# Pooled attention into a gated feed-forward layer: scores and main value products as single float32 matmuls, two product chains for the first tiles, a third weight buffer

## The chip, the core and the metric

The kernel runs on one core of a Trainium2 chip. TensorE (PE in the profile) multiplies: it holds a stationary operand of up to 128x128 and streams the columns of a moving operand past it, into PSUM. VectorE (DVE), ScalarE (ACT) and GpSimd (POOL) do the elementwise work; the SP queue issues all transfers between memory and SBUF. The metric is the device time of one execution in microseconds (us), as the median of the runs; it is compared with runs of the kernel before on the same chip.

## The reference

```python
def _attn_ref(q, k, v):                      # B, H, S, D = 8, 8, 576, 64
    k_p = k.reshape(B, H, 72, 8, D).mean(axis=3)
    v_p = v.reshape(B, H, 72, 8, D).mean(axis=3)
    scores = matmul(q, k_p.transpose(0, 1, 3, 2)) / sqrt(D)
    attn = exp(scores - max(scores))
    attn = attn / (sum(attn) + 1e-09)
    return matmul(attn, v_p)

x = attn_out.transpose(0, 2, 1, 3).reshape(4608, 512)
a, b = x @ w_a, x @ w_b                      # 512 x 1536 each
out = (a * b) @ w_out                        # 1536 x 512
```

All inputs are float32, and the weights arrive as 64-bit words that the kernel turns back into float32.

## The kernel before

**Tiles.** The 4608 rows of x are cut into 36 chunks of 128 rows, 18 blocks of 256 and 9 tiles of 512. A chunk goes through attention: scores (`psc`), softmax on DVE and ACT (`m`, `s`, `z`, `pr`), transposes on TensorE (`ptr`, `ptr_rem`); a block then has its value products (`po`), which are x transposed. The 64 first of the 72 pooled keys go through `vdiag`, the last 8 through `vrem`. A batch has 576 rows, so six of the 18 blocks lie in two batches, and so do chunks such as chunk 4. Keys and values of a batch are pooled by TensorE for batches 0 and 1 (`pkp`, `pvp`, true float32 matmuls with a matrix of eighths), by DVE otherwise.

**Feed-forward.** For each tile t and each of 12 slices f of the 1536 inner columns there is an inner product (`in`: `psa` and `psb`, 24 matmuls of 512 columns) and an outer one (`out`: `acc`, 12 matmuls). Tiles 0, 1 and 2 are done plainly; the pairs (3,4), (5,6), (7,8) with seven products in place of eight (`both`, banks `bank_psa`, `bank_psb`, `bank_att`).

**Split parts.** TensorE's float32r format keeps less of a number than float32. So each operand is split into a high part (a float32r copy, made by ACT) and a low part (the difference, made by DVE or POOL), and each product is three matmuls: high with high, high with low, low with high. This holds for the feed-forward products, and in the kernel before also for the scores (`qh`, `ql` from `qraw`; `kdiag` with two parts) and the main value products (`p0`, `p1`, in the first block `early_p`; `vdiag` with two parts).

**Weights.** For each f the words of w_a, w_b and w_out come in (`words`, 512 KB each), are converted in place on ACT and DVE (L500 to L520), split into `jab` (a and b) and `jo_open` (w_out), and the split parts are stored to memory (`jd`, `od`) for the later tiles. `jab` has two buffers, taken in turn.

**Order.** The order on each engine is made in advance by a list scheduler in the program (`Schedule`, with costs per operation): chains of operations are spawned with a rank, and among the operations that are ready on an engine at about the same planned time the lowest rank goes first. All feed-forward products of all tiles are one chain, `main`, in a fixed list `order`: in(0,f), then out(0,f-1), from f = 5 on with in(1,f) between them. On the chip each engine works strictly through its own list, and TensorE too starts its matmuls in that order. POOL may take a subtraction from DVE only after planned time `ALONE` (150 us), and when DVE's planned backlog exceeds `HELP`.

Of the kernel before, what the change touches and what calls it, by code (L numbers as in the profile page):

```python
# [17 lines left out]
POOL = 8  # L18
SP = S // POOL
P = 128  # L20
# [17 lines left out]
NTMP = 5  # L38
# [6 lines left out]
JOIN, STEP = 40, 8  # L45
# [16 lines left out]
MARGIN, HELP, AHEAD_F = 1.5, 1.5, 2  # L62
ALONE = 150.0
# [134 lines left out]
def attn_moe_kernel(ctx: ExitStack, tc: tile.TileContext, q, k, kn, v, vn, vr, wa, wb, wo, out):  # L198
# [79 lines left out]
    def pe(calls, rank=None, turn=False, passes=1):  # L278
        cost = 0.0
        for n, (to, lhs, rhs, *_) in enumerate(calls):  # L280
            cols = max(size(to), 64 if passes > 1 else 0) * passes
            other = n + 1 == len(calls) or (calls[n + 1][1].name, calls[n + 1][1].offset) != (lhs.name, lhs.offset)
            cost += max(COLUMN * cols, 0.075 if turn else 0.112 if other else 0.064)
# [25 lines left out]
    def xslot(x, name):  # L309
        return place(sb, [P, NK * NT], F32R, f"x{x}", name)  # L310
# [14 lines left out]
    work = place(sb, [P, 3 * 1024], I32, "work", "words")  # L325
    area = {"ab": work[:, :2048], "o": work[:, 2048:]}
# [11 lines left out]
    early_p = {x: xslot(x // 2, f"early_p{x}") for x in (0, 2)}  # L338
# [5 lines left out]
    jab = [jab_at(4 + x, f"jab{x}") for x in range(2)]  # L344
# [11 lines left out]
    def claim(tag):  # L356
        yield lambda: tag in banks
        banks.remove(tag)

# [243 lines left out]
    def sums_of_weights():  # L603
        yield W(*(("weight", name, NF - 1) for name in ("ab", "o")))
        three = place(sb, [P, 3, NK * BLOCK], F32R, "work", "sums")
        for f in range(NF):
            hi, lo = three[:, 2], three[:, f % 2]
# [129 lines left out]
    kv, qs = ["kv0", "kv1"], ["qraw"]  # L737
# [29 lines left out]
    def summed_keys(b):  # L767
        yield W(("keys", b - 1, 2), ("constants",))
        kd, tag = kdiag[b % 2], None
        for j in range(NK + 1):  # L770
            yield lambda: ("k", b, j) in raws
            if not j:
                tag = yield from take(banks)
                pt = bank(tag, f"pkp_{b}")[:, :NK * SP].rearrange("p (g s) -> p g s", g=NK)
# [5 lines left out]
            ], passes=4)  # L780
            kv.append(kv_of["k", b, j])
        for g0 in range(0, NK, 2):
            gs = slice(g0, g0 + 2)
            for e in range(2):
                r = slice(e * D, e * D + D)
                yield act(
                    kd[r, gs, 0, e, :], pt[r, gs], lambda r=r, e=e, gs=gs: nc.scalar.mul(kd[r, gs, 0, e, :], pt[r, gs], SCALE)
                )
            for e in range(2):
                r = slice(e * D, e * D + D)  # L790
                yield stt(kd[r, gs, 1, e, :], pt[r, gs], SCALE, kd[r, gs, 0, e, :].bitcast(F32), ALU.mult, ALU.subtract)
# [3 lines left out]
    def summed_values(b):  # L795
# [3 lines left out]
        for j in range(NK + 1):  # L799
            yield lambda: ("v", b, j) in raws  # L800
            rows, raw = rows_in(j), raws["v", b, j]
            if j in (0, NK):
                tag = yield from take(banks)
                pt = bank(tag, f"pvp_{b}_{j}")
            if j < NK:
                yield pe([(pt, main_of[:, j].rearrange("p e s -> p (e s)"), raw[:, :DM], not j, j == NK - 1)], passes=4)
            else:
# [5 lines left out]
                ], passes=4)  # L813
            if b:
                kv.append(kv_of["v", b, j])
            if j == NK - 1:
                by_pair = pt.rearrange("p (g e d) -> p g e d", g=NK, e=2)
                for e in range(2):
                    r = slice(e * KM, e * KM + KM)
                    yield copy(vd[r, :, 0, r], by_pair[r, :, e])  # L820
                for e in range(2):
                    r = slice(e * KM, e * KM + KM)
                    yield low_part(vd[r, :, 1, r], by_pair[r, :, e], vd[r, :, 0, r])
# [9 lines left out]
    def load_keys(b):  # L833
# [6 lines left out]
        for g0 in range(0, NK, 2):  # L840
# [10 lines left out]
            for e in range(2):  # L851
                r = slice(e * D, e * D + D)
                yield act(
                    kd[r, gs, 0, e, :], kp[r, gs],
                    lambda r=r, e=e: nc.scalar.mul(kd[r, gs, 0, e, :], kp[r, gs], SCALE / POOL),  # L855
                )
            for e in range(2):
                r = slice(e * D, e * D + D)
                yield stt(
                    kd[r, gs, 1, e, :], kp[r, gs], SCALE / POOL, kd[r, gs, 0, e, :].bitcast(F32), ALU.mult, ALU.subtract  # L860
                )
# [3 lines left out]
    def load_values(b):  # L865
# [12 lines left out]
        for e in range(2):  # L878
            r = slice(e * KM, e * KM + KM)
            yield act(  # L880
                vd[r, :, 0, r], vp[r, :NK], lambda r=r: nc.scalar.mul(vd[r, :, 0, r], vp[r, :NK], 1.0 / POOL)
            )
# [14 lines left out]
        for e in range(2):  # L897
            r = slice(e * KM, e * KM + KM)
# [529 lines left out]
```

## Time and profile before

| | before |
|---|---|
| median of 3 runs | 1019.37 us (1017.39 to 1020.46) |
| profiled execution | 1019.52 us |
| its span, first to last instruction | 1017.7 us |
| TensorE busy | 995.0 us (98%) |
| weight loads of TensorE busy | 829.3 us (81%) |
| VectorE busy | 623.9 us (61%) |
| ScalarE busy | 408.9 us (40%) |
| GpSimd busy | 172.0 us (17%) |
| mean granted TensorE clock | 0.983 |

TensorE's row is the one to read closely: a busy share of 98% does not tell at which clock it was busy, nor whether a matmul was bound by its columns or by the load of its stationary operand. Times of the prediction are counted against the profiled execution, which lies 0.15 us above the median.

### The profile page before, as it was taken

Reading aid. Unit: us, or ns where it says so; the run is one execution under the profiler, and the core shown is the slowest. Engines: PE = TensorE matmul, PEld = TensorE weight load, DVE = VectorE, ACT = ScalarE, POOL = GpSimd, SP = SyncE. Lnnn points to the kernel's source line nnn. Section 1 sums busy time; section 2 is a strip of 40 time slices with the busy share of each in tenths; the row PEclk is TensorE's granted clock in tenths of the full one; section 3 lists DMA queues with packets and bytes.
Section 4 is the critical chain, followed back from the end, with each engine's and each line's share of the span. In section 5 each row is a group of like instructions: output and inputs, shape, how many; then the busy total and the mean of one; then the engine's idle time right before and its main releaser. Section 6 shows DMA issues by size and latency. Waiting matters only on the chain.

```text
span 1017.7 us, 13575 instructions
## 1 busy us (share of the span) xinstructions
PE 995.0 (98%) x4824; PEld 829.3 (81%) x4824; DVE 623.9 (61%) x1018; ACT 408.9 (40%) x832; POOL 172.0 (17%) x139
## 2 busy tenths in 40 slices
PE   6889999999999999999999999999999999999998
PEld 5768888888888888888888887888888787888876
DVE  6697898889887885688776428333333733333331
ACT  5577755645465553544434215211111521111131
POOL 2000003201111110022212115022222502222210
PEclk9598999999999999999999999999999999999999
DMA  6396698798989789687775677666667967666792
GB/s 237 125 333 219 239 314 303 259 316 322 308 266 300 247 298 326 224 270 245 245 242 178 212 264 281 226 197 213 222 208 273 343 222 264 210 216 216 237 348 80
DMA packets 120659, 255.70 MB, mean 251 GB/s; under 512 B 10192, under 2 KB 26576, under 8 KB 120592
## 3 DMA queue, kind: packets, MB, share of 16 engines
q1 hardware_dynamic: 120592, 254.84, 74.3%
q8 instruction: 38, 0.62, 0.2%
q14 instruction: 29, 0.24, 0.1%
HBM read 195.30 MB, written 59.51 MB: 250 GB/s over the span
## 4 chain that ended last, share of the span: by engine, by line
PE 91%; DMA 4%; DVE 2%; ACT 1%; issue 0%; SPq 0%; POOL 0%; ACTq 0%
PE acc L291 28%; PE bank_psb L291 14%; PE bank_psa L291 10%; PE bank_att L291 9%; PE psa L291 9%; PE psb L291 9%; PE psc L291 5%; PE po L291 4%; PE ptr L288 1%; DMA words<-in_wb 1%; DMA j<-jd 1%; PE pvp L291 1%; PE pkp L291 1%; DMA kraw<-in_k 1%; DMA wo_first<-in_k 0%
## 5 line engine op out<-in xcount | busy, mean ns | idle before, releaser
L291 PE MATMUL bank_psb<-x,j 128*128 128x512 f32 x648 | 165.8, 391 | 0.8 <-DMA j<-jd 0.8
L291 PEld LDWEIGHTS bank_psb<-x,j 128*128 128x128 f32 x648 | 120.5, 188 | 26.2 <-DVE temp L234 1.2
L291 PE MATMUL acc<-jo_later,hh 128*128 128x512 f32 x384 | 121.3, 397 | 0.3
L291 PE MATMUL bank_psa<-x,j 128*128 128x512 f32 x432 | 110.8, 392 | 0.0
L291 PE MATMUL bank_att<-x,j 128*128 128x512 f32 x432 | 110.7, 391 | 0.0
L234 DVE TENSOR_TENSOR temp<-bank_psb,temp 128x512 f32<-128x512 f32 x72 | 49.8, 692 | 86.3 <-PE bank_psb L291 86.2
L291 PE MATMUL psa<-xh,jab 128*128 128x512 f32 x288 | 100.5, 402 | 0.0
L291 PE MATMUL psb<-xh,jab 128*128 128x512 f32 x288 | 99.3, 397 | 0.0
L291 PEld LDWEIGHTS bank_att<-x,j 128*128 128x128 f32 x432 | 80.3, 188 | 16.9 <-issue 0.4
L291 PEld LDWEIGHTS bank_psa<-x,j 128*128 128x128 f32 x432 | 80.3, 188 | 16.5
L234 DVE TENSOR_TENSOR temp<-bank_att,temp 128x512 f32<-128x512 f32 x54 | 37.3, 692 | 77.3 <-PE bank_att L291 74.9
L234 DVE TENSOR_TENSOR temp<-bank_psa,temp 128x512 f32<-128x512 f32 x54 | 37.3, 691 | 74.8 <-PE bank_psa L291 73.8
L291 PEld LDWEIGHTS acc<-jo_later,hh 128*128 128x128 f32 x384 | 69.5, 188 | 13.8 <-ACT hh L256 1.6
L234 POOL TENSOR_TENSOR temp_p<-temp_p,temp 128x512 f32<-128x512 f32 x36 | 46.9, 1302 | 194.2 <-ACT temp_p L256 189.2
L234 POOL TENSOR_TENSOR temp_h<-temp_h,temp 128x512 f32<-128x512 f32 x36 | 47.8, 1327 | 176.9 <-ACT temp_h L256 166.6
L291 PE MATMUL acc<-jo_later,hl 128*128 128x512 f32 x192 | 75.5, 393 | 0.6 <-DVE hl L234 0.6
L256 ACT CAST hh<-temp 128x512 fp32r<-128x512 f32 x36 | 22.4, 621 | 113.6 <-DVE temp L234 113.6
L291 PE MATMUL psc<-kdiag,qh 128*128 128x144 f32 x320 | 60.0, 283 | 8.2 <-ACT kdiag L855 8.0
L291 PEld LDWEIGHTS psc<-kdiag,qh 128*128 128x128 f32 x320 | 55.4, 200 | 14.8 <-POOL wab L442 8.0
L291 PEld LDWEIGHTS psa<-xh,jab 128*128 128x128 f32 x288 | 55.6, 193 | 11.3
L291 PE MATMUL acc<-jo_open,hh 128*128 128x512 f32 x192 | 61.9, 404 | 1.7 <-DVE wab L241 1.7
L291 PEld LDWEIGHTS psb<-xh,jab 128*128 128x128 f32 x288 | 54.1, 188 | 10.6
(156 smaller groups left out, 1850.1 us busy)
## 6 DMA issues: line engine op xcount, KB each, us to landing
j<-jd SPq DMA_DIRECT2D x108, 512.0 KB, 5.5
jo_later<-od SPq DMA_DIRECT2D x48, 512.0 KB, 3.7
wo<-od SPq DMA_DIRECT2D x36, 512.0 KB, 6.5
jab<-jd SPq DMA_DIRECT2D x34, 512.0 KB, 6.1
jd<-jab SPq DMA_DIRECT2D x24, 512.0 KB, 4.8
jd<-sums SPq DMA_DIRECT2D x24, 512.0 KB, 4.2
back<-later SPq DMA_DIRECT2D x43, 256.0 KB, 5.2
out<-y SPq DMA_DIRECT2D x36, 256.0 KB, 5.8
```

The source lines that it names most:

```text
L234: run = lambda e: vec[e].tensor_tensor(out=out, in0=in0, in1=in1, op=op)
L256: return act(out, in_, lambda: nc.scalar.copy(out, in_), rank)
L288: nc.tensor.transpose(to, lhs, rhs)
L291: nc.tensor.matmul(to, lhs, rhs, start=start, stop=stop, skip_group_check=bool(skip))
```

## The change

Three things are changed, and several numbers of the planner with them.

- Scores and main value products are one float32 matmul each, where three float32r matmuls stood. `qh`, `ql`, the low part of `kdiag`, the low part of `vdiag` and the low part of the transposed probabilities are gone, with the ACT copies of `q` and the DVE and POOL subtractions that made them. The products of the last 8 pooled keys (`vrem`) stay as they are.
- The products of tiles 0 and 1 are taken out of `main` into two chains: `first_ins` (inner products) and `first_outs` (outer products, with the better rank). `main` waits for the first and goes on with tile 2.
- `jab` has a third buffer. The raw q has three buffers in place of one, and there are 7 in place of 5 temporary tiles. The words of a and b and those of w_out get tiles of their own.

```diff
-NTMP = 5
+NTMP = 7
-JOIN, STEP = 40, 8
+JOIN, STEP = 40, 7
-MARGIN, HELP, AHEAD_F = 1.5, 1.5, 2
-ALONE = 150.0
+MARGIN, HELP, AHEAD_F = 1.5, 2.5, 2
+ALONE = 60.0
...
-    kdiag = [const.tile([P, NK, 2, 2, SP], F32R, name=f"kdiag{i}") for i in range(2)]
-    vdiag = [const.tile([P, NK, 2, P], F32R, name=f"vdiag{i}") for i in range(2)]
+    kdiag = [const.tile([P, NK, 2, SP], F32, name=f"kdiag{i}") for i in range(2)]
+    vdiag = [const.tile([P, NK, P], F32, name=f"vdiag{i}") for i in range(2)]
...
-    jab = [jab_at(4 + x, f"jab{x}") for x in range(2)]
+    jab = [jab_at(x, f"jab{n}") for n, x in enumerate((4, 5, 7))]
...
-        yield copy(qh, qraw)
-        yield low_part(ql, qraw, qh, (SG, SV))
...
                 yield pe([
-                    (
-                        pt[:, j * hk:(j + 1) * hk], qq[:, g0 + j], kd[:, g0 + j, w].rearrange("p e s -> p (e s)"),
-                        x == 0, x == 2,
-                    )
-                    for j in range(2) for x, (qq, w) in enumerate(((qh, 0), (qh, 1), (ql, 0)))
+                    (pt[:, j * hk:(j + 1) * hk], turned_q[:, g0 + j], kd[:, g0 + j].rearrange("p e s -> p (e s)"), True, True)
+                    for j in range(2)
                 ])
...
         yield copy(th[:, :, here], pt)
-        yield low_part(tl[:, :, here], pt, th[:, :, here])
...
-                        (vdiag[b % 2][:, g, 0, :], th[:, g, lo:hi], True, False),
-                        (vdiag[b % 2][:, g, 0, :], tl[:, g, lo:hi], False, False),
-                        (vdiag[b % 2][:, g, 1, :], th[:, g, lo:hi], False, False),
+                        (vdiag[b % 2][:, g], th[:, g, lo:hi], True, False),
...
+    def first_ins():
+        yield W(*(("value", block_of[i]) for i in range(NCH) if tile_of[i] == 0))
+        yield from claim("psa", "psb")
+        for kind, t, f in order:
+            if kind != "in" or t > 1:
+                continue
+            if t:
+                yield W(*(("value", block_of[i]) for i in range(NCH) if tile_of[i] == 1))
+            else:
+                mark("begun", f)
+            yield from ffn_in(t, f)
+            mark("issued", "in", t, f)
+        mark("first_ins")
+
+    def first_outs():
+        for kind, t, f in order:
+            if kind == "out" and t < 2:
+                yield from ffn_out(t, f)
+        ...
...
-        sch.spawn(main(), 1e9)
+        sch.spawn(first_outs(), 1e9)
+        sch.spawn(first_ins(), 2e9)
+        sch.spawn(main(), 2e9)
```

**Where the order changes.** Three places are shown, before and after. A name carries the chunk, block or batch and then a piece number, so `psc_4_2` is the second half of the scores of chunk 4, and `pvp_1_0` sums the values of batch 1 out of `vraw_1_0` to `vraw_1_3`; the last number of a name only keeps buffers apart.

On TensorE, before, the last value products of tile 0 are followed at once by the first inner product:

```order
L291 MATMUL po_1_2_488<-p0_1_427,vdiag0_79 128x256
L291 MATMUL po_1_2_488<-p2_1_429,vrem_0_214 128x256
L291 MATMUL psa_0_0_506<-xh_0_85,jab0_87 128x512
L291 MATMUL psa_0_0_506<-xl_0_86,jab0_87 128x512
L291 MATMUL psa_0_0_506<-xh_0_85,jab0_87 128x512 x2
```

The value sums of batch 1 and the scores of chunk 4 stand behind the inner product psa_0_1 there. On TensorE after, at the same place:

```order
L292 MATMUL po_1_2_423<-p2_1_369,vrem_0_193 128x256
L292 MATMUL pvp_1_0_432<-vraw_1_0_358,wab2_75 128x512
L292 MATMUL psc_4_0_428<-kdiag1_78,q_4_182 128x144 x2
L292 MATMUL pvp_1_0_432<-vraw_1_1_389,wab2_75 128x512
L292 MATMUL psc_5_0_429<-kdiag1_78,q_5_226 128x144 x2
L292 MATMUL psc_5_2_455<-kdiag1_78,q_5_226 128x144 x2
L292 MATMUL psc_4_2_465<-kdiag0_77,q_4_182 128x144 x2
L292 MATMUL psc_4_2_471<-kdiag1_78,q_4_182 128x144 x2
L292 MATMUL psc_6_0_478<-kdiag1_78,q_6_265 128x144 x2
L292 MATMUL psc_6_2_482<-kdiag1_78,q_6_265 128x144 x2
L292 MATMUL pvp_1_0_432<-vraw_1_2_440,wab2_75 128x512
L292 MATMUL pvp_1_0_432<-vraw_1_3_452,wab2_75 128x512
```

The main value sums of batch 1 and the scores of chunks 4, 5 and 6 moved ahead of the first inner product, which is the next row (psa_0_0).

On DVE, before, around the second half of tile 0 (`p1` is a low part that is gone after; `wab0` is the weight slice f = 0 until `jab0` is written, then f = 1; `xl` is the low part of x):

```order
L234 ISA wab0_73<-wab0_73,wlow_b0_283 128x1024
L245 TENSOR_SCALAR wo_first_72<-wo_first_72 128x512
L241 SCALAR_TENSOR_TENSOR wo_first_72<-words_82,wo_first_72 128x512
L234 TENSOR_TENSOR p1_1_428<-ptr_3_451,p0_1_427 128x4x128
L234 ISA wo_first_72<-wo_first_72,wlow_o0_322 128x1024
L234 TENSOR_TENSOR jab0_87<-wab0_73,jab0_87 128x2x512
L245 TENSOR_SCALAR wab0_73<-wab0_73 128x1024
L234 TENSOR_TENSOR xl_0_86<-po_1_0_472,xh_0_85 128x2x256
```

and after:

```order
L234 ISA wab0_73<-wab0_73,wlow_b0_336 128x1024
L245 TENSOR_SCALAR wo_first_72<-wo_first_72 128x512
L241 SCALAR_TENSOR_TENSOR wo_first_72<-words_o_83,wo_first_72 128x512
L234 ISA wo_first_72<-wo_first_72,wlow_o0_366 128x1024
L234 TENSOR_TENSOR jab0_88<-wab0_73,jab0_88 128x2x512
L234 TENSOR_TENSOR xl_0_87<-po_1_0_411,xh_0_86 128x2x256
```

The low part of the probabilities is gone between the weight steps, and the conversion of f = 1 moved behind the x of tile 0.

On the SP queue, before, the transfers around the first stores of split weights:

```order
L271 DMA jd0_90<-jab0_87 256x1x512
L271 DMA od0_102<-jo_open_89 128x1024
L271 DMA jd1_91<-jab1_88 256x1x512
L271 DMA words_82<-in_wo 128x1024
L271 DMA qraw_5_555<-in_q 128x512
L271 DMA vraw_1_2_591<-in_vn 128x512
L271 DMA jd1_91<-jab1_88 256x1x512
L271 DMA vraw_1_3_603<-in_vn 128x512
```

and after:

```order
L271 DMA vraw_1_1_389<-in_vn 128x512
L271 DMA words_o_83<-in_wo 128x1024
L271 DMA jd0_92<-jab0_88 256x1x512
L271 DMA od0_104<-jo_open_91 128x1024
L271 DMA vraw_1_2_440<-in_vn 128x512
L271 DMA vraw_1_3_452<-in_vn 128x512
```

The third and fourth value transfers of batch 1 moved ahead of the stores of f = 1, and stand right behind the first store of w_out's split parts (od0).

## Rows read from the trace of the kernel before

**Rows 1.** The page: TensorE's granted clock in 40 slices of the span, tenths.

```profile
PEclk9598999999999999999999999999999999999999
```

**Rows 2.** Busy time by stretch: PE, PEld, DVE, ACT, POOL, PEclk, DMA share, GB/s.

```profile
0.00:25.00 25.00, 16.14 (x74) 12.77 (x75) 17.27 (x37) 14.61 (x41) 6.47 (x19) 0.97 0.69 241
25.00:50.00 25.00, 21.33 (x93) 19.41 (x92) 16.83 (x34) 14.61 (x41) 0.00 (x0) 0.50 0.35 122
50.00:75.00 25.00, 22.21 (x110) 16.89 (x108) 22.48 (x40) 17.29 (x38) 0.00 (x0) 0.98 0.99 334
75.00:100.00 25.00, 23.31 (x123) 19.71 (x123) 19.84 (x37) 18.97 (x53) 0.00 (x0) 0.87 0.63 204
100.00:1000.00 900.00, 898.05 (x4372) 749.34 (x4371) 546.08 (x871) 339.83 (x655) 165.57 (x120) 1.00 0.77 258
```

**Rows 3.** The same view, of the two stretches at half clock.

```profile
23.60:50.90 27.30, 23.63 (x102) 21.52 (x102) 19.07 (x38) 15.96 (x44) 0.00 (x0) 0.50 0.34 116
74.80:81.60 6.80, 5.11 (x15) 3.75 (x14) 5.98 (x14) 4.98 (x17) 0.00 (x0) 0.50 0.57 203
```

**Rows 4.** The chain that ended last: start us, us, what, matmul records.

```profile
48.41 3.96 PE psa L291 x12
52.37 2.72 PE psb L291 x12
...
63.62 0.63 PE psc L291 x6
...
65.68 0.86 PE pvp L291 x2
...
90.38 1.76 PE po L291 x16
...
98.11 0.44 PE ptr L288 x4
...
114.32 0.12 PE ptr_rem L288 x2
...
117.25 0.95 PE po L291 x8
```

**Rows 5.** TensorE's groups by shape: count, busy us, mean ns, idle before and releaser.

```profile
L291 PE MATMUL psc<-kdiag,qh 128*128 128x144 f32 x320 | 60.0, 283 | 8.2 <-ACT kdiag L855 8.0 <-ACT xo L256 0.2
L291 PE MATMUL psc<-kdiag,ql 128*128 128x144 f32 x160 | 46.0, 287 | 0.9 <-DVE ql L234 0.9
L291 PE MATMUL po<-p,vdiag 128*128 128x256 f32 x132 | 23.9, 296 | 1.2 <-ACT p L256 0.8 <-DVE p L234 0.4
```

**Rows 6.** Timeline of TensorE in the opening: start us, us, what, records.

```profile
10.59 0.63 PE L291 MATMUL psc<-kdiag,qh 128*128 128x144 f32 x2
11.01 0.41 PE L291 MATMUL psc<-kdiag,ql 128*128 128x144 f32 x1
11.23 0.63 PE L291 MATMUL psc<-kdiag,qh 128*128 128x144 f32 x2
...
20.45 1.06 PE L291 MATMUL pkp<-eighth,kraw 128*128 128x16 f32 x8
21.37 0.42 PE L291 MATMUL psc<-kdiag,qh 128*128 128x144 f32 x2
```

**Rows 7.** Timeline of DVE in the opening, idle time and releaser in brackets.

```profile
33.06 0.69 DVE L234 TENSOR_TENSOR xl<-po,xh 128x512 fp32r<-128x512 f32 x1 [3.32 <-ACT xh L256]
38.39 0.69 DVE L234 TENSOR_TENSOR xl<-po,xh 128x512 fp32r<-128x512 f32 x1 [2.97 <-ACT xh L256]
```

**Rows 8.** Timeline of TensorE from 72 to 77 us.

```profile
74.38 0.69 PE L288 MATMUL ptr<-ident,pr 128*128 128x128 f32 x4 [2.54 <-DVE s L234]
76.75 0.79 PE L291 MATMUL acc<-jo_open,hh 128*128 128x512 f32 x1 [1.69 <-DVE wab L241]
```

**Rows 9.** Groups of DVE, ACT and POOL that the change removes: count, busy us, mean ns.

```profile
L234 DVE TENSOR_TENSOR p<-ptr,p 128x512 fp32r<-128x512 f32 x34 | 23.4, 689 | 17.4 <-ACT p L256 17.3
L256 ACT CAST qh<-qraw 128x512 fp32r<-128x512 f32 x32 | 19.9, 622 | 6.4 <-PE psc L291 3.6 <-DMA qraw<-in_q 2.5
L234 POOL TENSOR_TENSOR ql<-qraw,qh 128x512 fp32r<-128x512 f32 x19 | 26.0, 1369 | 114.4 <-ACT qh L256 88.5 <-PE po L291 16.6 <-DVE vdiag L241 5.6
```

**Rows 10.** Transfers issued from 25 to 100 us: count, KB each, median us to landing.

```profile
words<-in_wb SPq DMA_DIRECT2D x5, 512.0 KB, 5.2
vraw<-in_vn SPq DMA_DIRECT2D x4, 256.0 KB, 4.2
```

More of the change, by code (lines that the diff above doesn't have):

```diff
@@ L276, in until_ready, with pe @@
         return op
-    def pe(calls, rank=None, turn=False, passes=1):
+    def pe(calls, rank=None, turn=False):
         cost = 0.0
         for n, (to, lhs, rhs, *_) in enumerate(calls):
-            cols = max(size(to), 64 if passes > 1 else 0) * passes
+            exact = lhs.dtype == F32 and not turn
             other = n + 1 == len(calls) or (calls[n + 1][1].name, calls[n + 1][1].offset) != (lhs.name, lhs.offset)
-            cost += max(COLUMN * cols, 0.075 if turn else 0.112 if other else 0.064)
+            floor = 0.225 if exact else (0.109 if lhs.dtype == F32 else 0.061) if turn else 0.111 if other else 0.068
+            cost += max(COLUMN * size(to) * (4 if exact else 1), floor)
         def run(e):
@@ L819, in summed_values @@
                     r = slice(e * KM, e * KM + KM)
[L820 to L823, printed above, removed]
+                    yield copy(vd[r, :, r], by_pair[r, :, e])
                 banks.append(tag)
@@ L853, in load_keys @@
                 yield act(
[L854 to L860, printed above, removed]
+                    kd[r, gs, e], kp[r, gs], lambda r=r, e=e: nc.scalar.mul(kd[r, gs, e], kp[r, gs], SCALE / POOL)
                 )
@@ L896, in load_values @@
         yield copy(vrf[:NR], wide[:NR])
-        for e in range(2):
-            r = slice(e * KM, e * KM + KM)
-            yield stt(vd[r, :, 1, r], vp[r, :NK], 1.0 / POOL, vd[r, :, 0, r].bitcast(F32), ALU.mult, ALU.subtract)
         r = slice(2 * 4 * KR, NR)
@@ L957, in chunk @@
                     banks.append(tag)
+        if not first:
+            qs.append(tag_q)
         for n, (tag, four) in enumerate(held_banks):
@@ L1308, in both @@
         waiting.extend(ffn_out(t0, f, (c,)) for c in range(NT // P))
+    def first_ins():
[15 more added lines that the diff above has]
+                yield from ffn_out(t, f)
+        jo.append(place(sb, [P, 4 * 512], F32R, "jo", "jo_later").rearrange("p (k h c) -> p k h c", k=2, h=2))
+        mark("first_outs")
     def main():
+        yield W(("first_ins",))
         for kind, t, f in order:
[L1312 to L1321 removed]
+            if kind == "in" and t > 1:
+                yield W(("whole", t))
                 yield from ffn_in(t, f)
                 mark("issued", "in", t, f)
[L1324 removed]
+            elif kind == "out" and t > 1:
+                yield W(("first_outs",))
                 yield from ffn_out(t, f)
[L1326 to L1327 removed]
             elif kind == "both":
                 yield from both(t, f)
[L1330 removed]
+            elif kind == "rest":
                 while waiting:
```

105 lines of the change are left out of this document (42 added, 63 removed).

## The prediction

> **What bounds the kernel now.** I read the busy time by stretch first, because a share of 98% over the whole span says nothing about single stages. From 100 to 1000 us TensorE is busy 898.05 of 900 us at a granted clock of 1.00 [rows 2]: there only the price of its own matmuls counts, and what the other engines are spared costs or gains nothing as long as they stay ahead (DVE 546 of the 900 us, ACT 340). The first 100 us are another matter: TensorE is busy 16.1, 21.3, 22.2 and 23.3 of 25 us each, and in two stretches, 23.6 to 50.9 and 74.8 to 81.6 us, at half clock [rows 1 to 3]. I then read the chain that ended last for the price of a matmul, as start to start in a row of its kind: 12 feed-forward matmuls take 2.72 us, so 0.227 each; six score matmuls 0.63, so 0.105; a float32 value sum (pvp, two records of 512 columns) 0.86; eight value matmuls of 256 columns 0.95; sixteen of a block in two batches 1.76; four transposes 0.44, two small ones 0.12 [rows 4]. The mean durations of single matmuls (283 ns for a score) are no price, since matmuls overlap [rows 5]. Three terms follow: TensorE's own work, the opening up to the first inner product, and the stretch after it.
>
> **Term 1, TensorE's own work.** Scores: 480 matmuls now, in 80 groups of six [rows 5], at 0.63: 50.4 us. After, 160 float32 matmuls of 144 columns. The trace has float32 matmuls at two sizes. At 512 columns one takes 0.86, that is 1.68 ns a column, which gives 0.242 for 144. At 16 columns eight records (four matmuls) take 0.92 us from 20.45 to 21.37, so 0.23 a matmul [rows 6]; this is the floor, and 0.242 lies just above it. 160 x 0.242 = 38.7: a gain of 11.7 us. Bounds: the score stays at 0.242 if load and stream overlap as in these rows; some 0.01 for changing between kinds would leave 10.
>
> Here a rule of the Trainium skill speaks against the change. By the row, three float32r matmuls of 144 columns take 0.315, and the width sets little of it, as 256 columns take hardly more (0.95/8 = 0.119) [rows 4]. The Trainium skill's page FP8 and Floating Point Precision, section TensorE Precision Notes, says that true float32 takes four passes through the array, so by columns alone four passes replace three. By that count three matmuls would cost 3 x 144 x 0.227/512 = 0.19, and the change would lose about 8 us on the scores in place of gaining 11.7. The trace agrees on the four passes (0.86 against 0.227 for 512 columns) but not on the count by columns, and the Trainium skill's page TensorE: Matmul & The Clock Gate, section LDWEIGHTS (loading the stationary operand), has the reason: a load of the stationary operand takes time by its own 128 columns, an estimate of 107 ns by its formula, whatever streams past it. Since the rows price the three matmuls directly, the count by columns gets no chance of its own below.
>
> Value products: 12 blocks lie in one batch. There a group of two head pairs has eight matmuls at 0.95; after it has two float32 ones at 256 x 1.68 ns = 0.43 and two for the rest at 0.119, 1.10 in all: +0.15 x 24 = +3.6 us. In the six blocks with two batches sixteen matmuls take 1.76; after, pieces of 64 and 128 columns cost the floor of 0.23 and 192 columns 0.32, and the rest 0.11 each: 1.54 (64 with 192, four blocks) or 1.36 (128 with 128, two). That is -0.22 x 8 - 0.40 x 4 = -3.4. Together nothing. Term 1 is -11.7, say -12, between -9 and -13.
>
> **Term 2, the opening.** The first inner product (psa) starts at about 48.2 us [rows 4]. TensorE began at 8.0, when the first kdiag was there [rows 5], and waits and half clock filled the rest. After, TensorE's list ahead of psa is at full clock: 32 score matmuls 7.7, eight value sums of 512 columns 6.9 and four small ones 0.9, 20 key sums 4.6, four chunks of transposes 2.2, eight head pairs of value products at 0.55 4.4; 26.7 us. Of this, 7.3 us (four value sums, 16 score matmuls) stood behind the first psa before. So the term is the shift of psa plus 7.3.
>
> When does psa start? With TensorE never waiting: 8.0 + 26.7, and 4.4 more since it ran at half rate up to some 17 us (three scores in 0.64 at 10.6 us, against 0.315 later [rows 4, 6]): 39. With half clock for all that is left at 23.6 us: 15.5 x 2, so 55. Between the ends: the stretch at half clock held key sums, whose streams are 16 columns wide, and pieces broken by waits; the clock came back at 50.9, 2.7 us after the dense psa began [rows 3, 4]. After, the list ends in a dense run of float32 products (po_1, value sums, scores, some 10 us at full clock), in which it should come back too, while key sums, transposes and po_0 (6 us) stay at half. That gives 45. It needs the others to keep up. DVE had gaps of 3.3 and 3.0 us there, waiting for x through TensorE's cold key sums [rows 7], and loses about 7 us of work ahead of psa: four ql and four low parts of p at 0.69 or less, the low kdiag and vdiag [rows 9]. What is late next is the value transfer vraw_1_2: it waits for its buffer (the first value sum) and behind the od0 store, takes 4.2 us to land [rows 10], and psa stands behind it; between lie seven groups of scores, 3.4 us, and one value sum, 0.86, so it costs at most a microsecond or two. Term 2: (48.2 - 45) + 7.3 = -10.5, between -16.5 (39) and -0.5 (55).
>
> **Term 3, 50 to 100 us.** Here TensorE stood idle 2.8 and 1.7 us and ran 6.8 us at half clock with 5.1 busy [rows 2, 3], a loss of about 4.5 + 2.5 = 7. The large waits are for chunk 4's softmax (2.54 us at the transpose) and a bank behind DVE's weight step (1.69) [rows 8]; DVE was busy 22.5 of 25 us. After, chunk 4's scores stand ahead of psa, its transposes in the fourth half product behind it (some 15 us later), and each chunk spares DVE or POOL two subtractions [rows 9], so these waits go. What is late next is the weights: each slice f moves 3 MB (three transfers of 512 KB in, three out), and at the 334 GB/s of a full DMA [rows 2] that is 9.4 us, while TensorE needs 36 x 0.227 = 8.2 us a slice plus some 3 of attention. That is balance, with words landing after 5.2 us [rows 10]; the third jab buffer lets a split run ahead of the products, but not ahead of the words. I take 4 of the 7 us back; bounds -7 and +4 (a new wait for weights, as psa comes sooner).
>
> After 100 us nothing else changes: the ACT copies and POOL subtractions removed there (20 and 26 us [rows 9]) lay beside a full TensorE. Sum, against the profiled execution's 1019.5 us (0.15 above the median of the runs, so the same number stands for both): 1019.5 - 12 - 10.5 - 4 = 993.
>
> **The rivals.** (a) The weights pace the start: TensorE reaches the inner products sooner and waits there for f = 1 to 3, since DMA is at 99% from 50 to 75 us [rows 2]. Terms 2 and 3 then cancel, and term 1 is left: 1007. Against it: DMA is at 35% from 25 to 50 us, so there is room to start sooner. (b) All goes well: psa at 39 and 7 us back in term 3: 1019.5 - 12 - 16.5 - 7 = 984. (c) Slower: load and stream of a float32 record add up in place of overlapping where the stream is short. A score record is then 0.115 + 0.121 = 0.236, 320 of them 75.5, +25 us; the 192 records of the value products cost about 0.115 x 192 = 22 more; with terms 2 and 3 the time is 1052. It decides from a record of 0.2 us on, where the scores alone eat terms 2 and 3. Against it: two records of 512 columns in 0.86 leave no room for loads [rows 4]. (d) No change: the opening stays cold to the end (term 2 is -0.5) and psa's turn brings new waits of 9 to 14 us that eat term 1, in the in-order list behind vraw and the split weights: 1017 to 1022.
>
> **How the numbers follow.** Forecast 993 with a chance of 0.65, (a) 0.15, (b) 0.13, (c) 0.04, (d) 0.03. A measurement of this kernel can tell about 0.3%, 3 us, from no change. Faster by more: forecast, (a) and (b), 0.93; within: (d), 0.03; slower: (c), 0.04. The range goes from (b)'s 984, a little wider, to just past (a)'s 1007: 983 to 1009.
>
> **What would show it.** Six scores become two float32 matmuls in about 0.49 us in the chain, against 0.63. psa starts at 45 us, with the clock back before it; a start after 50 would break term 2. From 50 to 100 us TensorE's idle time falls below 3 us and no half clock remains; a wait of psa for jab or words would show (a). From 100 us on TensorE is full as before; if it is not, the freed engines were not ahead after all and the forecast is wrong in a place that I counted at nothing.

## The result, and the profile of the changed kernel

The changed kernel takes 987.44 us (median of 4 runs, 986.57 to 989.27), the kernel before 1019.25 (1017.39 to 1020.46) beside it: a ratio of 0.9692, with a 95% interval of 0.9672 to 0.9712. Forecast were 993.0 and a range of 983 to 1009. The profiled execution took 987.53 us, its span 985.7, 32.0 less than before.

The page of the changed kernel gives the busy time of each engine and TensorE's granted clock in 40 slices:

```profile
PE 968.0 (98%) x4568; PEld 801.7 (81%) x4568; DVE 560.6 (57%) x928; ACT 387.9 (39%) x796; POOL 126.4 (13%) x109
PEclk9899999999999999999999999999999999999999
```

The busy time by stretch, with the columns of [rows 2]:

```profile
0.00:25.00 25.00, 17.09 (x92) 13.99 (x92) 16.38 (x35) 14.02 (x53) 4.69 (x19) 1.00 0.76 266
25.00:50.00 25.00, 21.17 (x106) 16.25 (x106) 21.15 (x38) 18.41 (x38) 0.00 (x0) 0.86 0.80 270
50.00:75.00 25.00, 24.60 (x127) 20.49 (x126) 23.10 (x43) 21.99 (x70) 0.00 (x0) 1.00 0.93 313
75.00:100.00 25.00, 24.87 (x123) 20.51 (x122) 21.91 (x37) 20.04 (x45) 5.17 (x3) 1.00 0.84 296
100.00:960.00 860.00, 858.25 (x4031) 712.72 (x4030) 474.62 (x774) 308.09 (x587) 116.55 (x87) 1.00 0.79 261
```

Against [rows 2] the second stretch has a clock of 0.86 in place of 0.50, and from 50 us on TensorE is busy and at full clock. After 100 us it was so before as well, so nearly all that was gained there must be the price of TensorE's own work (the account below has 8.1 us lost there before and 6.8 after).

The chain that ended last, some rows from the opening to 123 us (start, us, what, records), answers to [rows 4]:

```profile
26.42 2.42 DMA kraw<-in_kn
...
38.79 2.94 PE psc L292 x24
41.73 0.87 PE pvp L292 x2
42.60 0.02 issue
42.62 4.74 DMA vraw<-in_vn
...
72.56 1.53 PE po L292 x12
...
93.15 1.10 PE po L292 x6
...
122.64 0.49 PE psc L292 x4
```

Four score records (two float32 products) take 0.49, the value products of a block group 1.10 and 1.53: these prices came out as forecast. TensorE's timeline around its first inner product (idle time and releaser in brackets) shows what is still waited for:

```profile
28.88 1.05 PE L292 MATMUL pkp<-eighth,kraw 64*128 64x8 f32 x8 [0.55 <-DMA kraw<-in_kn]
...
44.28 0.50 PE L292 MATMUL psa<-xh,jab 128*128 128x512 f32 x1 [0.84 <-ACT vdiag L256]
...
47.41 1.11 PE L292 MATMUL pvp<-vraw,wab 64*96 64x128 f32 x8 [1.49 <-DMA vraw<-in_vn]
```

psa starts at 44.28 us, and the transfer of the values costs 1.49 us inside it. The low clock of the opening is one stretch:

```profile
30.00:36.80 6.80, 6.34 (x19) 4.95 (x20) 4.94 (x8) 5.00 (x10) 0.00 (x0) 0.50 0.94 332
```

**What a group takes out of the row.** A row of the chain runs from the end of the matmul ahead of a group to the end of the group's last one (122.64 to 123.13 above), and so leaves out what the matmuls behind the group pay. A cleaner measure is from the start of the last 512-column matmul ahead of a group to the start of the third behind it, less 3 x 0.227. TensorE's timeline of before, around six scores:

```profile
155.06 0.39 PE L291 MATMUL psb<-xh,jab 128*128 128x512 f32 x1
155.28 0.34 PE L291 MATMUL psc<-kdiag,qh 128*128 128x144 f32 x2
...
155.91 0.67 PE L291 MATMUL acc<-jo_open,hh 128*128 128x512 f32 x2
156.42 0.40 PE L291 MATMUL acc<-jo_open,hl 128*128 128x512 f32 x1
```

and of the changed kernel, around two float32 scores:

```profile
122.25 0.39 PE L292 MATMUL psa<-xh,jab 128*128 128x512 f32 x1
122.48 0.65 PE L292 MATMUL psc<-kdiag,q 128*128 128x144 f32 x4
122.88 0.49 PE L292 MATMUL psa<-xh,jab 128*128 128x512 f32 x1
123.20 0.39 PE L292 MATMUL psa<-xl,jab 128*128 128x512 f32 x1
123.43 0.40 PE L292 MATMUL psa<-xh,jab 128*128 128x512 f32 x1
```

Before, 156.42 - 155.06 - 0.68 = 0.68; after, 123.43 - 122.25 - 0.68 = 0.50. Over all groups that stand alone, the medians are 0.684 (41 groups) and 0.505 (22). In the same way eight value matmuls of 256 columns cost 0.98 before and the four that replace them 1.13; a block group in two batches 1.80 before, 1.55 or 1.36 after.

**An account of the span.** With these prices (and 0.227 for each 512-column matmul of float32r, 0.43 a record of a value sum, 0.46 for four transposes, the smaller kinds likewise) each trace splits into TensorE's own work at full clock and lost time, which is idle time and half clock together: the time passed, less the prices of the matmuls that began in it. It is worked out from all matmul records of a trace, so its rows are sums and not rows of a view, and own work is a count times a price: a price that is wrong would show as lost time. It holds for the profiled execution, which in e1 lies 1.8 us above the median of the runs, in e2 5.2 below it, and elsewhere within 2. To the last matmul, in us:

| kernel | median | psa starts | work ahead of it | own work | lost ahead of psa | lost psa to 100 | lost after 100 |
|---|---|---|---|---|---|---|---|
| before | 1019.3 | 48.2 | 21.2 | 969.6 | 27.0 | 8.8 | 8.1 |
| changed | 987.4 | 44.3 | 27.8 | 955.2 | 16.4 | 3.1 | 6.8 |
| e1 products only | 999.6 | 38.7 | 23.1 | 955.2 | 15.6 | 8.5 | 16.2 |
| e2 values only | 1031.5 | 39.5 | 21.8 | 969.5 | 17.7 | 20.2 | 12.9 |
| e3 scores only | 1009.1 | 50.2 | 27.3 | 955.3 | 22.9 | 10.8 | 14.2 |
| e4 one chain | 998.4 | 43.6 | 27.8 | 955.2 | 15.7 | 10.9 | 9.9 |
| e5 two jab | 992.9 | 42.7 | 27.8 | 955.2 | 14.8 | 5.6 | 12.2 |
| e6 old numbers | 992.5 | 43.8 | 27.8 | 955.2 | 15.9 | 5.8 | 10.5 |
| e7 inner first | 996.8 | 44.0 | 27.8 | 955.2 | 16.2 | 3.1 | 14.8 |
| e8 three kv | 989.7 | 40.4 | 25.0 | 955.2 | 15.4 | 5.8 | 7.8 |
| e9 VectorE pass | 996.0 | 51.9 | 29.0 | 955.2 | 22.9 | 5.2 | 6.9 |
| e12 three kv, three q | 993.7 | 35.5 | 25.0 | 955.2 | 10.6 | 10.8 | 9.7 |

The change is -14.4 in own work, -10.6 ahead of psa, -5.7 from there to 100 us and -1.3 behind: -32.0. The experiments ask what made each.

### The profile page after: what moved, and what is told of

The parts are those of the page before. It is cut to its first block, busy times and chain, and to the rows that moved or that the text cites. A ratio compares the mean times of both kernels' runs of the same rounds, so it can differ in the third digit from the quotient of the medians.

```text
span 985.7 us, 12862 instructions
## 1 busy us (share of the span) xinstructions
PE 968.0 (98%) x4568; PEld 801.7 (81%) x4568; DVE 560.6 (57%) x928; ACT 387.9 (39%) x796; POOL 126.4 (13%) x109
## 4 chain that ended last, share of the span: by engine, by line
PE 92%; DMA 4%; ACT 2%; DVE 1%; issue 1%; SPq 0%; ACTq 0%
PE acc L292 29%; PE bank_psb L292 15%; PE bank_psa L292 10%; PE bank_att L292 10%; PE psb L292 9%; PE psa L292 9%; PE po L292 4%; PE psc L292 4%; PE ptr L289 1%; PE pvp L292 1%; DMA j<-jd 1%; DMA jd<-sums_high 1%; DMA kraw<-in_kn 1%; DMA q<-in_q 0%; DMA vraw<-in_vn 0%
## 5 line engine op out<-in xcount | busy, mean ns | idle before, releaser
L292 PEld LDWEIGHTS bank_psa<-x,j 128*128 128x128 f32 x432 | 80.8, 188 | 16.8
L292 PE MATMUL psb<-xl,jab 128*128 128x512 f32 x144 | 56.3, 391 | 0.0
L292 PE MATMUL psa<-xl,jab 128*128 128x512 f32 x144 | 56.2, 390 | 0.0
```

Of the source, the lines that this page charges most:

```text
L292: nc.tensor.matmul(to, lhs, rhs, start=start, stop=stop, skip_group_check=bool(skip))
```

## The experiments

All ratios stand against runs of the kernel before on the same chip, as medians with 95% intervals; on the chips used that kernel took 1019.25 to 1019.95 us, so times may be compared as well. Except for e2, e3, e10 and e11, every kernel has the changed kernel's matmuls. Where a kernel's operations or ranks differ, the list scheduler plans the whole order anew, so a difference of two or three us between two such kernels can be another order rather than the edit.

### e1 to e3: which products

e1 is the changed kernel without its new order and buffers; e2 and e3 are e1 with one kind of product split again. All kernels below but e10 also keep three lesser things of the change that no run undoes: separate tiles for the words of a and b and of w_out, a claim of the banks of psa and psb together (`claim("psa", "psb")`), and the planner's new prices for TensorE's operations.

```
e1  one chain `main` as before; jab (4, 5, 7) -> (4, 5); q0, q1, q2 -> q0; NTMP 7 -> 5; STEP, HELP, ALONE as before
e2  e1, and per head pair  (qh, kd0), (qh, kd1), (ql, kd0)  in place of  (q, kd)
e3  e1, and per head pair  (vd0, th), (vd0, tl), (vd1, th)  in place of  (vd, th)
```

> The float32 products alone, on the order of before: one chain of inner and outer products, two jab buffers, the scheduler's old numbers, one query buffer, five temporaries. Theory (the products themselves bring most): TensorE's own work falls by 14.5 us (80 groups of scores from 0.684 to 0.505, value products at no net change), and since DVE and POOL are spared the low parts, part of the lost time of the first 100 us comes back as well, some 8 us: 997 us, between 992 and 1001. Rival (the order and the buffer bring all that was gained ahead of 100 us): the opening and the 50 to 100 us stretch stay as before, only the 14.5 us come: 1005, and the clock still drops in 24 to 50 us as before.

> As e1, but with the scores split again into three float32r products, so that only the value products are float32. Theory by insertion counts: TensorE's own work stands as before (value products cost +3.7 us in twelve blocks and give 3.8 back in six), so after 100 us nothing changes; DVE is spared the low part of p, which gives a few us in the opening: 1012 to 1019. The difference to e1 is the price of the scores, 14.4 us by the insertion count (0.684 against 0.505), 11.2 by the chain's rows (0.63 against 0.49), plus what the opening gets. Rival (the float32 value product overlaps worse than its row says, e.g. by 0.1 us in each of 144 head pairs): 10 us slower than that.

> As e1, but with the value products split again into three float32r products and one for the rest, so that only the scores are float32. Theory: TensorE's own work is that of e1, the time lies 0 to 6 us above e1, by what DVE's low parts of p cost in the opening: 997 to 1005. If value products in float32 are a loss on TensorE that other relief hid, this kernel is faster than e1; if they are a gain, it is slower by more than 6 us.

Measured: e1 999.59 us, ratio 0.9792 (0.9759 to 0.9826); e2 1031.51, 1.0105 (1.0066 to 1.0144); e3 1009.08, 0.9900 (0.9873 to 0.9926).

e1 bears out its theory: the products, with the three things just named, give 20 of the 32 us. In the account 14.4 are own work and 11.4 come ahead of psa (27.0 to 15.6), and 8.1 are lost again after 100 us. So the opening needs neither the chains nor the third buffer.

e2 missed its expectation by 12 us, on the slow side; its five executions spread from 1025 to 1035 us, and the profiled one (1026.3) misses by 7. Its own work is what was expected (969.5 against 969.6), and ahead of psa it loses 9.3 less than before. But it then loses 20.2 us up to 100, with a clock of 0.72 from 50 to 75 us. The measured time is near that of its rival, a dearer float32 value product (the trace has 96 of them, not 144), but the trace rules this rival out: a group of four value matmuls takes 1.13 in e2 as in the change (median of 17 groups). e3 missed as well, 4 us beyond its range: it lies 9.5 us above e1 by the medians and 7.7 by the profiled executions, of which the account puts +9.6 ahead of 100 us (22.9 + 10.8 against 15.6 + 8.5), -2.0 behind, and nothing into own work. The stretches of e2 (first three rows) and of e3 (the last), columns as above, and the wait with which e2's long stretch at half clock begins:

```profile
25.00:50.00 25.00, 21.89 (x119) 18.38 (x119) 22.13 (x41) 18.90 (x43) 0.00 (x0) 0.93 0.74 245
50.00:75.00 25.00, 20.27 (x89) 15.99 (x87) 22.44 (x40) 20.54 (x57) 0.00 (x0) 0.72 0.90 304
61.20:91.90 30.70, 26.26 (x95) 22.43 (x95) 24.17 (x50) 23.27 (x79) 0.00 (x0) 0.50 0.80 268
```

```profile
25.00:50.00 25.00, 21.45 (x98) 17.92 (x98) 18.90 (x33) 15.73 (x34) 0.00 (x0) 0.70 0.60 192
```

```profile
61.03 1.90 PE L292 MATMUL pvp<-vraw,wab 64*96 64x128 f32 x8 [2.75 <-DMA vraw<-in_vn]
```

What differs in the opening is the clock: with the value products in float32 (e2) it is 0.93 there, with the scores alone (e3) 0.70. All the gain in own work comes from the scores. Ahead of psa, splitting the values again costs 7.3 us against e1 (22.9 against 15.6) and splitting the scores 2.1 (17.7), so most of the gain in the opening comes from the value products; the other 2 of e1's 11.4 may belong to the three things that all these kernels keep. Why e2 stood so long for vraw, and at half clock for 30.7 us after it, was not tried.

### e9: is that VectorE's relief?

The value products spare VectorE the low parts of p and vdiag, and the products a wait for them. e9 gives back those of p and of the vdiag of the two batches that TensorE pools, and leaves TensorE's products as they are:

```diff
         yield copy(th[:, :, here], pt)
+        yield tt(th[:, :, here], pt, th[:, :, here], ALU.min, (SV,))
         banks.append(tag)
...
                     yield copy(vd[r, :, r], by_pair[r, :, e])
+                for e in range(2):
+                    r = slice(e * KM, e * KM + KM)
+                    yield tt(vd[r, :, r], by_pair[r, :, e], vd[r, :, r], ALU.min, (SV,))
```

> The changed kernel, with VectorE spending on every p and every vdiag what it spent on their low parts before: it reads the bank and the copy of ScalarE once more (a minimum of the two, in place, which alters nothing), and the products wait for it; TensorE's products stay those of the change. Of the changed products, e2 (values in float32 alone) lost 17.7 us ahead of the first inner product, e3 (scores alone) 22.9, before 27.0 and the change 16.4. Theory (the value products help the opening through what VectorE is spared): 20 to 24 us are lost ahead of the first inner product, and the time is 3 to 8 us longer than the change, 990.5 to 995.5. Rival (they help by TensorE's own denser products and the clock): 16 to 18 us are lost there, and the time is within 3 us, 986 to 991.

Measured: 995.98 us, ratio 0.9768 (0.9746 to 0.9790); 22.9 us lost ahead of psa. A stretch of e9, and two waits in its TensorE timeline:

```profile
25.00:50.00 25.00, 22.84 (x100) 18.85 (x100) 16.74 (x31) 14.72 (x34) 0.00 (x0) 0.70 0.50 164
```

```profile
23.74 1.22 PE L292 MATMUL po<-early_p,vdiag 128*128 128x256 f32 x2 [1.48 <-DVE early_p L234]
...
49.53 1.96 PE L292 MATMUL pvp<-vraw,wab 64*96 64x128 f32 x8 [2.16 <-DVE wab L234]
```

The theory holds: the lost time is in its range (20 to 24), the time half a microsecond beyond it. With float32 products on TensorE but VectorE loaded as before, 6.5 of the 10.6 us ahead of psa are lost again, the clock from 25 to 50 us is 0.70 as in e3, and psa starts at 51.9. The first row shows the direct wait, for a product standing behind the pass over p; the second an indirect one, TensorE behind a step of VectorE's conversion of weights that ends at 49.4 us here and ended at 41.5 in the change. Much of the loss is clock: it is half from 22.3 to 39.3 us here, against 30.0 to 36.8 in the change. VectorE itself is busy only 16.74 of these 25 us: it is no bound by its share, but it stands at several places in a series of steps (scores, softmax, transpose, p, product, x). The other 4.1 us no run undoes; e3, which has the scores' relief without that of the values, loses 22.9 as well, 4.1 less than before. Some 2 of them stand at the very start of the program, as the last section shows.

### e4 to e6: chains, buffer, numbers

Each undoes one part of the changed kernel:

```
e4  first_ins and first_outs back into main's fixed list
e5  jab = ... enumerate((4, 5, 7))  ->  enumerate((4, 5))
e6  STEP 7 -> 8, HELP 2.5 -> 1.5, ALONE 60 -> 150
```

> The changed kernel with its inner and outer products of the first two tiles as one chain again, in the fixed order of before; third weight buffer, queries in three buffers and the new numbers stay. Theory (two chains matter only while weights or banks are late, and TensorE loses little after its first inner product): 0 to 3 us slower than the change, 987 to 990.5. Rival (the two chains let outer products fill waits between 50 and 100 us, which was term 3): 4 to 7 us slower, 991.5 to 994.5, with TensorE idle or at half clock between 50 and 100 us.

> The changed kernel with two weight buffers (jab) for the inner products in place of three; two chains and all else stay. Theory (the third buffer only lets a split run ahead; the words are not late from 50 to 100 us): within 3 us of the change, 986 to 991. Rival (the two chains can run ahead of one another only because the third buffer is there): the gain of the two chains, 11 us, is lost again, 995 to 999, with 8 to 11 us lost between the first inner product and 100 us in place of 3.

> The changed kernel with the scheduler's old numbers (STEP 8, HELP 1.5, ALONE 150); products, chains and buffers stay. In e1 and e4, which have other numbers and buffers, 16.2 and 9.9 us are lost after 100 us against 6.8 in the change and 8.1 before. Theory (the numbers decide what is lost after 100 us): 5 to 8 us slower than the change, 992 to 996, lost after 100 us. Rival (the buffers decide that, and the numbers are fine tuning): within 3 us, 986 to 991.

Measured: e4 998.43 us, ratio 0.9798 (0.9771 to 0.9826); e5 992.93, 0.9733 (0.9695 to 0.9772); e6 992.50, 0.9732 (0.9699 to 0.9766).

e4 is 11 us slower, past even its rival. Between 60 and 75 us TensorE stands as follows, in e4:

```profile
60.00:65.00 5.00, 2.75 (x12) 1.99 (x12) 4.73 (x9) 4.63 (x14) 0.00 (x0) 0.87 0.94 294
65.00:70.00 5.00, 3.62 (x11) 2.10 (x9) 4.49 (x11) 4.40 (x21) 0.00 (x0) 0.50 0.88 270
70.00:75.00 5.00, 5.00 (x19) 4.14 (x19) 3.53 (x7) 3.25 (x6) 0.00 (x0) 0.61 0.95 321
```

and in the changed kernel:

```profile
60.00:65.00 5.00, 5.00 (x28) 4.21 (x28) 4.89 (x11) 4.67 (x13) 0.00 (x0) 1.00 0.89 272
65.00:70.00 5.00, 4.60 (x23) 3.52 (x22) 4.90 (x11) 3.74 (x13) 0.00 (x0) 1.00 0.94 320
70.00:75.00 5.00, 5.00 (x30) 4.43 (x30) 4.33 (x8) 4.16 (x12) 0.00 (x0) 1.00 0.97 298
```

TensorE's timeline of e4 in this stretch, its waits and what comes then:

```profile
63.09 0.80 PE L292 MATMUL psc<-kdiag,q 128*128 128x144 f32 x4 [2.12 <-ACT p L256]
...
68.17 1.22 PE L292 MATMUL acc<-jo_open,hh 128*128 128x512 f32 x2 [0.82 <-ACT s L264]
...
71.36 0.63 PE L292 MATMUL psa<-xh,jab 128*128 128x512 f32 x1
```

From 60 to 70 us DVE (4.73 and 4.49 of 5 us) and ACT are nearly full in both kernels. In e4 the third inner product stands behind the outer product of the first slices, whose operands come late from ACT; it starts at 71.4 us, on a halved clock. In the changed kernel it starts at 60.3, ahead of all but the first three matmuls of the outer product, and fills the time. So the stretch after psa owes its gain first of all to the two chains: 10.9 us are lost in e4, 3.1 in the change. Without them it would even be worse than before (8.8).

e5 lies 5.5 us above the change, between its theory and its rival; e6 5.1, as its theory has it, though not only behind 100 us. Of e5 and e6, 2.5 and 2.7 us are lost from psa to 100 us and 5.4 and 3.7 after it, less 1.6 and 0.5 that they gain ahead of psa. Both intervals still reach into that of the change (0.9672 to 0.9712), so these five microseconds are less sure than the eleven of e4. The single steps don't add up: taking the chains alone away (e4) costs 11.0, taking chains, buffers and numbers away together (e1) 12.2. With the chains gone, buffers and numbers are worth 1.2 us, so their five microseconds, if they are real, need the two chains.

### e7, e8 and e12: can the opening still give something?

```
e7   sch.spawn(first_ins(), 2e9)  ->  sch.spawn(first_ins(), 30.0)
e8   kv = ["kv0", "kv1"]  ->  ["kv0", "kv1", "kv2"];  q0, q1, q2 -> q0, q1
e12  kv as in e8, q0 to q2 kept, NTMP 7 -> 6
```

> The changed kernel with its chain of inner products ranked ahead of the work of attention, so that the first inner products, once their x and weights are there, don't stand back behind value sums and scores of the next tile. Theory (the work that was moved ahead of the first inner product fills time that is lost there anyway, and lost time ahead of it stays near 16 us): the same time as the change or up to 8 us slower, 987 to 996, since attention comes later and the products of the second tile wait for it. Rival (moving work ahead only delays the first inner product): 1 to 4 us faster.

> The changed kernel with three buffers for raw keys and values in place of two (and two for the queries in place of three, to make room). In the change TensorE waits for key and value transfers three times ahead of the first inner product and 1.5 us inside it; vraw waits for a buffer to come free. Theory (these transfers pace the opening): 3 to 7 us come back, 980 to 985. Rival (the transfers are paced by the DMA itself, busy 76 to 93% of the first 75 us, so that a buffer only moves the wait): within 3 us of the change, 985 to 991.

> As e8, three buffers for raw keys and values, but with the queries' three buffers kept and one temporary less. In e8 the waits for key and value transfers went, psa started at 40.4 us, and 2.4 us were lost again at a transpose at 57 us, where chunk 5 was late. Theory (a query buffer less made that): 983 to 987. Rival (each order that the scheduler finds loses a few us in another place): 987 to 992.

Measured: e7 996.83 us, ratio 0.9775 (0.9740 to 0.9810); e8 989.71, 0.9700 (0.9660 to 0.9739); e12 993.71, 0.9749 (0.9718 to 0.9780).

The times of e7 and e12 lie beyond what was expected, 0.8 us above e7's theory and 1.7 above e12's rival; e8 lies in the range of its rival.

e7 says nothing on the work ahead of psa: that stayed 27.8 us and psa at 44.0, probably since x isn't there any sooner, whatever the rank. It lost 14.8 us after 100 us instead, 6.2 of them from 250 to 300.

e8 and e12 remove the waits for the keys' transfers, e8 also that for the values' (e12 still waits 1.17 us for them, behind its first psa). In e12 the opening goes as well as it ever did: psa at 35.5, 10.6 us lost ahead of it, and the clock at 1.00 from 25 to 50 us. Then it loses 10.8 us up to 100. Its stretches, and two waits of TensorE:

```profile
25.00:50.00 25.00, 22.72 (x124) 18.04 (x124) 22.75 (x38) 21.61 (x53) 0.00 (x0) 1.00 0.89 303
...
75.00:100.00 25.00, 21.93 (x103) 18.16 (x103) 21.11 (x36) 19.06 (x44) 1.58 (x1) 0.93 0.87 295
```

```profile
53.22 0.50 PE L292 MATMUL psa<-xh,jab 128*128 128x512 f32 x1 [0.95 <-ACT jab L256]
...
79.31 1.22 PE L292 MATMUL acc<-jo_open,hh 128*128 128x512 f32 x2 [3.07 <-ACT s L264]
```

psa at 53.2 waits for jab on ACT, and an outer product at 79.3 for 3.07 us behind ACT's softmax. The first is the wait of the prediction's rival (a), in a kernel that reaches the inner products 9 us sooner; the longer one is not for weights. DVE and ACT are busy 22.75 and 21.61 of 25 us from 25 to 50, and what the opening gives, the conversion of weights and above all the softmax take back. Neither kernel is faster than the change, so a better opening alone is not worth a buffer here.

### e10 and e11: the price of a score

Both issue the list of a score group twice (times is 2 there, 1 elsewhere):

```diff
-            for to, lhs, rhs, *more in calls:
+            for to, lhs, rhs, *more in calls * times:
```

> The kernel before, with each group of score products issued twice over into the same bank (the result is the same), 480 matmuls more, in the same order otherwise. Theory A (a group of six costs 0.63 for its matmuls, and 0.054 for the change to another kind of product, once a group): +50.4 us at full clock, 1070, of which the opening may add a few. Theory B (each of the six costs a sixth of the 0.684 that a group takes out of the row of 512-column products): +54.7, 1074. The prediction's step rests on 0.63; inserted groups of six more should measure 1.31 under A and 1.37 under B.

> The changed kernel with each pair of float32 score products issued twice over (the result is the same), 160 float32 products more. Theory: a float32 product of 144 columns costs 0.245 (the chain's row 0.49 for two), and the change of kind almost nothing more (0.505 a group), so +39.2 us at full clock: 1027, and a group of four products takes 0.995 out of the row of 512-column ones. Rival (load and stream of the two records add up when float32 products stand in a longer row): 0.47 or more a product, +75.

Measured: e10 1075.14 us, ratio 1.0550 (1.0531 to 1.0569); e11 1023.07, 1.0039 (1.0027 to 1.0051), or 35.6 us above the changed kernel. TensorE's timeline of e10, around twelve scores:

```profile
113.83 0.40 PE L291 MATMUL psb<-xh,jab 128*128 128x512 f32 x1
114.06 0.34 PE L291 MATMUL psc<-kdiag,qh 128*128 128x144 f32 x2
...
115.36 0.67 PE L291 MATMUL acc<-jo_open,hh 128*128 128x512 f32 x2
115.86 0.39 PE L291 MATMUL acc<-jo_open,hl 128*128 128x512 f32 x1
```

and of e11, around eight records (four float32 products):

```profile
130.76 0.39 PE L292 MATMUL psa<-xh,jab 128*128 128x512 f32 x1
130.98 1.14 PE L292 MATMUL psc<-kdiag,q 128*128 128x144 f32 x8
131.87 0.49 PE L292 MATMUL psa<-xh,jab 128*128 128x512 f32 x1
132.19 0.39 PE L292 MATMUL psa<-xl,jab 128*128 128x512 f32 x1
132.43 0.39 PE L292 MATMUL psa<-xh,jab 128*128 128x512 f32 x1
```

Twelve float32r scores take 115.86 - 113.83 - 0.68 = 1.35, where theory B expected 1.37 and A 1.31: six more cost 0.67, or 0.111 each, not 0.105. The time agrees: +55.2 us, where 80 x 0.667 is 53.4 and the prediction's price would give 50.4. Four float32 products take 132.43 - 130.76 - 0.68 = 0.99: two more cost 0.485, so 0.242 a product, as forecast. Of the 38.8 us that this makes, e11 shows 35.6. The account of its trace places the missing 3: it loses 1.1 us less than the change ahead of psa and 2.1 less from there to 100 us, where more scores fill time that is lost otherwise. In e10 it is the other way round, 3.2 us more are lost ahead of psa.

## Why the prediction was right, and where not

**Term 1, TensorE's own work: too small, -12 for -14.4.** The comparison is as written: three float32r scores cost more than one float32 score. The step that failed is the price of the six scores. "Six score matmuls 0.63, so 0.105 each" was read off the chain [rows 4] as start to start, but its rows run from end to end. The two 512-column matmuls behind such a group take 0.51 (155.91 to 156.42 in the timeline above) in place of 0.454, which the chain books on them. In the row the six cost 0.684, and e10 shows that the marginal price is 0.667. 80 x (0.684 - 0.505) is 14.3. The float32 side (0.242, e11) and the value products' zero (+0.15 x 24 against -0.25 x 8 and -0.44 x 4; e2's own work 969.5) came out. The gain lies 1.4 beyond the term's bound of -13. What sets the 0.242 the runs can't tell at this width: it is 144 columns at 1.68 ns, and hardly above the 0.23 that 16 columns take [rows 6].

The Trainium skill's page FP8 and Floating Point Precision, section TensorE Precision Notes, speaks of four passes for float32. As the prediction had it, this case's runs agree on the passes (0.86 for 512 columns, 3.8 times 0.227) and not on a price by columns: by that, the split scores of e2 would be some 8 us less work than the float32 ones of e1, and they are 14.3 us more.

**Term 2, the opening: right in size, -10.5 for -10.6, in part by luck.** psa at 44.3 was forecast at 45, the work moved ahead of it is 6.6 us for 7.3. But what the 45 was added up from missed in both directions. Behind the first 8 us the forecast took 26.7 of work, 4.4 lost at the half pace of the start, 6 at half clock, and no waits. The trace has 27.8 of work, about 2.5 lost at the start (7.9 to 12.9 us), about 3.2 at half clock (30.0 to 36.8) and 2.3 of waits (0.8 of them for kraw, 0.8 for vdiag). The wait for vraw, 1.49 for "a microsecond or two", came behind the start of psa, at the small value sums, and not at vraw_1_2. The step that failed is "key sums, transposes and po_0 (6 us) stay at half": with three buffers for keys and values (e12) the clock does not fall in the opening at all, with the same key sums. Beside it stood a VectorE that only has to keep up, and that did not hold either: with its passes over p and vdiag given back (e9), 6.5 us come back as loss, and the clock falls to 0.70. The gaps of 3 us on DVE [rows 7] had been read as DVE waiting for TensorE; each waits for the other in turn, and a pass taken out of this series is a gain although the engine has gaps. Too much for the clock and the start, and nothing for the waits: the sum fitted by that.

**Term 3, 50 to 100 us: -5.7 for -4, for another reason.** The waits of [rows 8] did go (one of 0.40 us is left from 50 to 100), and the weights did not come late. But the step "chunk 4's scores stand ahead of psa, so these waits go" does not explain the gain: e4 has the same products, 27.8 us of work ahead of psa and the third buffer, and loses 10.9 us there, in other waits, all for ACT (2.12, 0.82 and 0.46 us), and at half clock. The two chains, a part of the change that the prediction gave no price, carry the term: without them (e4) the kernel is 11.0 us slower, 7.8 of them in this stretch.

**After 100 us**, counted at nothing, 1.3 us were gained. Nothing is not a safe price there either: e1 and e7 lose 16.2 and 14.8 us after 100, 5.6 and 6.2 of them in a single stretch of 50 us (550 to 600, and 250 to 300). Both stretches have waits for DVE or ACT (3.84 us in e1, 1.00 and 1.33 in e7), and beside them 6.8 us at half clock, with TensorE busy through all of it in e7.

**The rivals.** (a) did not come about in the change; e12, with psa at 35.5 us, shows its wait for jab, though only 0.95 us of it. (b) went halfway: 5.7 of its 7 us in term 3, but psa at 44.3 and not at 39. (d) did not come about, the clock was back at 36.8 us. (c), load and stream of a float32 record adding up, is ruled out by e11, where eight records in a row cost 0.124 each.

## What to carry to other kernels

A group of short matmuls between long ones is priced over the matmuls behind it too: from the last long one ahead to the third behind, less what these take alone. In a stage where several engines hand one small piece of work to each other, the passes that a change removes from the series can count in full and more, however idle the engine looks (in e9, 3.6 us of passes ahead of psa cost 6.5); and where one list holds work that waits and work that doesn't, letting the second go ahead (two chains here) can be worth nearly as much as the arithmetic. Before a gain is booked to the arithmetic, undo the order alone: here it was 11 of 32 us.

## What was not expected of the hardware

The 512-column matmul behind a group pays for the change of kind: 0.32 us after two float32 scores (122.88 to 123.20) against the 0.227 that it takes behind its own kind, and two of them 0.51 after six float32r scores, against 0.454.

At the very start a row of the view misleads. In the changed kernel, the first sixteen score records begin at 7.91 us and the next group at 11.88, so four of them take 0.99, for what takes 0.49 later. TensorE has no gap in this time, and the view gives a clock of 1.00:

```profile
7.90:12.10 4.20, 4.19 (x17) 4.20 (x18) 2.11 (x4) 1.96 (x10) 0.00 (x0) 1.00 1.06 348
```

But the trace holds no granted clock for this stretch. Its first record of the clock begins at 12.93 us (16.79 in the kernel before), and the view counts time without a record as full. The pace changes there too: a score record takes 0.24 us up to 11.9 us and 0.12 from 15.0 on. So the start ran at half the later pace; at which level the clock stood no row shows. The first record begins at 16.8 us or later in the three traces with split scores (before, e2, e10), and between 10.4 and 13.0 in all the others. Half of 16.8 - 8.0 against half of 12.9 - 7.9 is 1.9 us, a part of the opening's gain that goes with the scores; why the pace rose sooner was not tried.
